# Oct 0's compact channels by staging copy and DMA transpose in difference form, with the DMA rates in the scheduler's model raised

## Chip, cores and metric

One core of a Trainium2 chip. The metric is the device time of one execution in microseconds (us), the median of several runs.

## The reference

A dilated causal convolution over time with a gated activation and a projection:

```python
# x (2, 16000, 144), w (15, 144, 288), w_o (144, 144), all bf16
dil, pad = 2, 28
xp = pad x with 28 zero rows ahead in time
h = sum over i in 0..14 of xp[:, pad - 2*i : pad - 2*i + T, :] @ w[i]     # 288 columns
z = tanh(h[..., :144]) * sigmoid(h[..., 144:])
return z @ w_o
```

## The kernel before

The 32000 time steps lie on 128 partitions, 250 steps each. One step of all partitions is a "tile" (128 rows); eight tiles are an "oct". The matmuls need the channels on the partitions, so every tile is transposed: channels 0 to 127 into XA, one tile each, and the last 16 channels ("compact channels", kept in XBc) packed eight taps to a 128-row tile, into XB. For fewer matmuls, differences of tiles and sums of weights are formed first (V, DU, DD, GU, GD, GX, GV from XA; WS, WC, WT from the weights), in the manner of a fast convolution.

All instructions are collected as operations with an estimated duration. A list scheduler inside the kernel's builder simulates the five engines and one DMA resource, and its simulated starts become the order in which each engine's instructions are emitted. An estimate in that model therefore never changes what is computed, but it changes the order.

Short names used below: "WS,GU matmuls" are those with WS as weights and GU as data; "XA<-STA" is an operation that reads STA and writes XA; a "bank copy" is a copy within PS, the accumulator memory; SPq and ACTq are the DMA queues of SyncE and ScalarE; ZT is the transposed Z, and OS holds the output before it is stored.

```python
DMA_RATE = 280e3
...
            if op.dma:                                   # in the scheduler's simulation
                t0 = max(dma_free, st + op.dur)
                turn = op.dma in ("xa", "xb", "zt")      # the DMA transposes
                dma_free = t0 + op.nbytes / (DMA_RATE * (0.6 if turn else 1.0))
                op.end = dma_free + (0.6 if turn else 2.3 if op.dma in ("xp", "wa", "wb") else 1.3)
...
        # compact channels of octs -1 and 0: TensorE transposes, ScalarE eviction
        for o, tiles, bb in ((-1, range(E0 - 4, E0), 7), (0, range(E0, E0 + 8), 6)):
            ...
            g.add("pe", fns, r=hk5 + ["XBcz", "ID"], alloc=[bk], dur=0.06 * len(fns))
            xb_op = g.add("act", ... activation(XB[:, bslot(o), i0:8, :], PSb[...], ACT.Copy), ...)
...
        def load_xb(o, parts=(0, 1)):                    # octs 1 and later
            for h in parts:
                def cp(v, h=h):                          # staging: XBc -> STB, 128x768
                    ...
                    return v.tensor_copy(dst, src) if o in BDVE else v.activation(dst, src, ACT.Copy)
                g.add("dve" if o in BDVE else "act", cp, ...)
            return g.add("sp", lambda e: e.dma_start_transpose(XB[:, s, :, :], STB[:, q, :, :]...),
                  r=[("STB", q, 0), ("STB", q, 1)], w=[("XB", s)], dur=1.7, dma="xb", ...)
```

"Staging" also exists for XA: a copy of Xr (the loaded x) into STA and a DMA transpose of 8 tiles. SyncE issues these transposes, the loads of Xr and the output stores from one queue, strictly in order.

## Time and profile before

| | before |
|---|---|
| time, median of 3 runs | 321.55 us (320.90 to 322.44) |
| span of the profiled run | 319.0 us |
| TensorE matmuls and transposes | 2643 in the profile, 2645 in the program |
| 100 to 280 us | TensorE never rests, full clock |

The profile is read in two layers. The page says who is busy; the chain and the starts of TensorE's instructions say who waits for whom. The lines that this rests on stand in the prediction below. One definition is used from here on. A **hole** is the time between the start of a group of TensorE instructions and the moment at which it could have started, which is the start of the group before it plus 0.123 us for each 288-column matmul in that group (0.057 us for each 128-column transpose).

### The profile page before, as it was taken

Reading aid. Unit: us, or ns where it says so; the run is one execution under the profiler, and the core shown is the slowest. Engines: PE = TensorE matmul, PEld = TensorE weight load, DVE = VectorE, ACT = ScalarE, POOL = GpSimd, SP = SyncE. Lnnn points to the kernel's source line nnn. Section 1 sums busy time; section 2 is a strip of 40 time slices with the busy share of each in tenths; the row PEclk is TensorE's granted clock in tenths of the full one; section 3 lists DMA queues with packets and bytes.
Section 4 is the critical chain, followed back from the end, with each engine's and each line's share of the span. In section 5 each row is a group of like instructions: output and inputs, shape, how many; then the busy total and the mean of one; then the engine's idle time right before and its main releaser. Section 6 shows DMA issues by size and latency. Waiting matters only on the chain.

```text
span 319.0 us, 6912 instructions
## 1 busy us (share of the span) xinstructions
PE 310.7 (97%) x2643; PEld 239.1 (75%) x2643; DVE 284.6 (89%) x615; ACT 267.5 (84%) x635; POOL 16.6 (5%) x29
## 2 busy tenths in 40 slices
PE   7999999999999999999999999999999999999994
PEld 6677667777777777777777777777777777777673
DVE  2999999999999998999989999898989989894774
ACT  3896699898897989989798897979889797788674
POOL 8106400000000000000000000000000000000000
PEclk9999999999999999999999999999999999999999
DMA  8699969949987592988949495894949477131553
GB/s 206 209 207 165 266 117 218 179 128 183 194 165 197 105 245 73 209 165 122 251 92 238 94 205 156 147 210 108 229 111 183 100 131 184 46 69 74 113 131 92
DMA packets 127821, 50.38 MB, mean 158 GB/s; under 512 B 119134, under 2 KB 121615, under 8 KB 127789
## 3 DMA queue, kind: packets, MB, share of 16 engines
q1 hardware_dynamic: 127273, 49.62, 74.1%
q0 software_dynamic: 512, 0.33, 0.4%
q8 instruction: 20, 0.33, 0.4%
q14 instruction: 12, 0.10, 0.1%
q10 hardware_dynamic: 4, 0.01, 0.0%
HBM read 11.82 MB, written 9.22 MB: 66 GB/s over the span
## 4 chain that ended last, share of the span: by engine, by line
PE 86%; ACT 7%; DMA 4%; SPq 1%; issue 1%; DVE 0%; ACTq 0%
PE PS L747 76%; PE PS L846 9%; DMA XA<-STA 2%; ACT STB L680 2%; DMA Xp<-in_x_dram 2%; ACT STA L659 1%; ACT TS L768 1%; SPq L479 1%; ACT TS L771 1%; ACT PS L905 1%; ACT XB L620 0%; SPq L491 0%; PE PS L579 0%; PE PS L877 0%; ACT XA L588 0%
## 5 line engine op out<-in xcount | busy, mean ns | idle before, releaser
L1026 DVE TENSOR_TENSOR Xp<-PS,UX 128x576 f32<-128x576 f32 x90 | 63.0, 751 | 16.7 <-PE PS L747 16.6
L747 PE MATMUL PS<-WB,XB 128*128 128x288 bf16 x260 | 72.1, 286 | 0.0
L1038 DVE TENSOR_TENSOR PS<-PS,Xp 128x576 f32<-128x576 f32 x90 | 68.4, 760 | 2.1 <-ACT OS L854 1.0
L747 PE MATMUL PS<-WA,GD 128*128 128x288 bf16 x360 | 70.0, 286 | 0.1
L768 ACT ACTIVATE TS<-PS 128x288 f16<-128x288 f32 x125 | 51.7, 413 | 13.3 <-PE PS L747 12.3
L854 ACT ACTIVATE OS<-PS 128x432 bf16<-128x432 f32 (+1 forms) x88 | 42.3, 489 | 14.0 <-PE PS L846 12.8
L771 ACT ACTIVATE TS<-PS 128x288 f16<-128x288 f32 x125 | 51.4, 411 | 0.0
L905 ACT ACTIVATE PS<-PS 128x288 f32<-128x288 f32 x120 | 46.3, 408 | 2.8 <-PE PS L747 2.8
L974 ACT ACTIVATE UX<-PS 128x576 f32<-128x576 f32 x60 | 39.2, 654 | 10.7 <-PE PS L747 10.4
L680 ACT ACTIVATE STB<-XBc 128x768 bf16<-128x768 bf16 x56 | 47.5, 854 | 0.0
L747 PE MATMUL PS<-WS,GU 128*128 128x288 bf16 x210 | 44.3, 287 | 0.0
L846 PE MATMUL PS<-WOR,ZT 128*128 128x144 bf16 (+1 forms) x322 | 42.4, 253 | 0.2 <-DVE Xp L1026 0.2
L747 PEld LDWEIGHTS PS<-WA,GD 128*128 128x128 bf16 x360 | 33.7, 98 | 11.4 <-DVE PS L1038 3.2
L776 DVE TENSOR_TENSOR Z<-TS 128x288 bf16<-128x288 f16 x125 | 36.9, 301 | 4.4 <-ACT TS L771 4.2
L747 PE MATMUL PS<-WC,XB 128*128 128x288 bf16 x120 | 34.3, 286 | 0.0
L846 PEld LDWEIGHTS PS<-WOR,ZT 128*128 128x128 bf16 x322 | 27.9, 98 | 6.6 <-ACT OS L854 0.5
L747 PE MATMUL PS<-WD,DD 128*128 128x288 bf16 x180 | 31.9, 286 | 0.2 <-ACT PS L905 0.2
L747 PE MATMUL PS<-WC,V 128*128 128x288 bf16 x180 | 30.6, 286 | 0.0
L747 PE MATMUL PS<-WA,DD 128*128 128x288 bf16 x180 | 30.6, 286 | 0.0
L747 PEld LDWEIGHTS PS<-WB,XB 128*128 128x128 bf16 x260 | 25.4, 98 | 6.7 <-ACT XB L620 0.3
L747 PE MATMUL PS<-WA,V 128*128 128x288 bf16 x118 | 25.7, 286 | 0.3 <-ACT PS L1111 0.3
L747 PE MATMUL PS<-WT,DU 128*128 128x288 bf16 x120 | 24.5, 286 | 0.0
(93 smaller groups left out, 459.4 us busy)
## 6 DMA issues: line engine op xcount, KB each, us to landing
Xr<-in_x_dram SPq DMA_DIRECT2D x15, 576.0 KB, 4.6
out_dram<-OS SPq DMA_DIRECT2D x30, 288.0 KB, 3.0
WA<-in_w_dram SPq DMA_DIRECT2D x3, 288.0 KB, 5.3
ZT<-Z SPq DMA_TRANSPOSE x32, 3.7
Xp<-in_x_dram SPq DMA_DIRECT2D x2, 252.0 KB, 5.4
XA<-STA SPq DMA_TRANSPOSE x30, 3.5
XB<-STB SPq DMA_TRANSPOSE x30, 4.4
Xp<-in_x_dram SPq DMA_DIRECT2D x1, 441.0 KB, 4.1
```

Of the source, the lines that this page charges most:

```text
L479: return e.dma_start(tile_ap, src)
L680: return v.tensor_copy(dst, src) if o in BDVE else v.activation(dst, src, ACT.Copy)
L747: return lambda t: t.matmul(bank(bk.b), lhsT=lhs(), rhs=rhs(), start=start, stop=True, skip_group_check=True)
L768: return a.activation(TS[:, s, 0, :, :], both(bk, 0, D), ACT.Tanh)
L771: return a.activation(TS[:, s, 1, :, :], both(bk, D, D), ACT.Sigmoid)
L776: return v.tensor_tensor(dst, TS[:, s, 0, :, :], TS[:, s, 1, :, :], ALU.mult)
L846: return t.matmul(PS[:, c0:c0 + n * D], lhsT=ZT[:, zt, blk, :], rhs=WOR[:, wi:wi + n, :].rearrange("p a b -> p (a b)"), start=first, stop= ...
L854: return e.tensor_copy(dst, src) if eng == "dve" else e.activation(dst, src, ACT.Copy)
L905: g.add("act", lambda e: e.activation(bank(bk.b + 1), bank(bk.b), ACT.Copy), w=[bk], dur=t_act(N2), prio=0)
L974: g.add("act", lambda e: e.activation(UX[:, k, u % NU, :, :], both(X, 0, N2), ACT.Copy), r=[X], w=[("UX", k, u % NU)], frees=[X], dur=t_ac ...
L1026: g.add("dve", lambda v, k=k, wi=wi, vb=vb, us=us: v.tensor_tensor(wslot(wi), both(vb, 0, N2), UX[:, k, us, :, :], ALU.add), r=[vb, ("UX", ...
L1038: return v.tensor_tensor(both(d, 0, N2), src, wslot(wi), ALU.add)
```

## The change

Its intent: oct 0 is treated like all later octs. The 8 TensorE transposes and the eviction go, two ScalarE copies and one DMA transpose of 12 tiles come. The matmuls of oct 0's outputs must then use the difference form (tiles already subtracted on XBc, and one shared tile), and the shared one is added to each output tile apart. Besides, the model's DMA rate for transposes rises from 0.6 to 0.68 of DMA_RATE.

```diff
-                dma_free = t0 + op.nbytes / (DMA_RATE * (0.6 if turn else 1.0))
+                dma_free = t0 + op.nbytes / (DMA_RATE * (0.68 if turn else 1.0))
...
+    SHX = ()
...
-        for o, tiles, bb in ((-1, range(E0 - 4, E0), 7), (0, range(E0, E0 + 8), 6)):
+        for o, tiles, bb in ((-1, range(E0 - 4, E0), 7),):
...
-        def direct_b(k, b):
-            e = H + k
-            g.add("pe", region(b, [lambda: xb_tile(e), lambda: xb_tile(e - 2)], [lambda: WB[:, 0, :], lambda: WB[:, 1, :]]), ...)
+        def rem(k, shared_too=True):
+            ...
+            out = [(lambda: XB[:, bslot(o), bb + (2 if j == 0 else 0) + r, :], (lambda: WB[:, 0, :]) if j == 0 else (lambda: WC[:, 2, 3, :]))]
+            if shared_too:
+                out.append((lambda: XB[:, bslot(o), bb + 4 + r, :], lambda: WB[:, 2, :]))
+            return out, [...]
+        def direct_b(k, b, shared_too=True):
+            tw, keys = rem(k, shared_too)
+            g.add("pe", region(b, [x[0] for x in tw], [x[1] for x in tw]), r=keys, w=[b.bk], ...)
+        g.add("act", lambda a: a.activation(WC[:, 2, 3, :], WB[:, 1, :], ACT.Copy, scale=-1.0), ...)   # moved up
+        diff_b("dve", 1, 9, hk5 + ["XBcz"], "XBd_h")                                                   # was ("dve", 3, 7, ...), later
+        load_xb(0)
...
+            if pi == 0 and q in SHX:              # an option of the kernel, off here: share one matmul of a pair
+                tw, keys = rem(k_of(q))
+                g.add("pe", region(_Half(bk, 0), [tw[1][0]], [tw[1][1]]), ...)
```

Cut: the slices that let load_xb serve oct -1 too, the choice of tiles in rem, moved lines, and two ordering constraints that tied the pair sums to the old eviction and are dropped.

## The prediction

> **What bounds the kernel now.** I read the page first (busy shares, the chain), then the windows, then the chain in order of time, and last the instructions of TensorE between 13 and 47 us. The page:
>
> ```profile
> PE 310.7 (97%) x2643; PEld 239.1 (75%) x2643; DVE 284.6 (89%) x615; ACT 267.5 (84%) x635; POOL 16.6 (5%) x29
> ...
> PE 86%; ACT 7%; DMA 4%; SPq 1%; issue 1%; DVE 0%; ACTq 0%
> ```
>
> TensorE is busy 97% of the span and carries 86% of the chain that ended last. The stretches say where the rest lies (columns: busy us and instructions of PE, PEld, DVE, ACT, POOL, then clock, DMA share, GB/s):
>
> ```profile
> 15.00:20.00 5.00, 5.00 (x41) 3.52 (x39) 5.00 (x17) 5.00 (x11) 0.00 (x0) 1.00 0.87 202
> 20.00:25.00 5.00, 4.67 (x39) 3.50 (x38) 4.70 (x13) 5.00 (x11) 0.00 (x0) 1.00 0.96 183
> 25.00:30.00 5.00, 5.00 (x43) 3.92 (x41) 5.00 (x14) 3.25 (x9) 3.27 (x6) 1.00 1.05 128
> 30.00:35.00 5.00, 5.00 (x43) 3.99 (x41) 4.86 (x9) 2.50 (x6) 5.00 (x11) 1.00 1.26 229
> ...
> 100.00:200.00 100.00, 100.00 (x843) 77.11 (x842) 93.81 (x202) 88.52 (x213) 0.00 (x0) 1.00 0.77 163
> 200.00:280.00 80.00, 80.00 (x678) 61.94 (x677) 74.18 (x153) 69.43 (x168) 0.00 (x0) 1.00 0.72 145
> ```
>
> From 100 to 280 us TensorE never rests at full clock; the chain shows there only pieces of "PE", with a period of 9.37 us (a 7.90 us piece begins at 99.67 + 9.37 = 109.04, and so on). Nothing but fewer matmuls can shorten that part. Waits are left in the first 50 us, where ScalarE is full from 15 to 25 us and the DMA engines from 15 to 40. There the chain is:
>
> ```profile
> 12.36 1.02 ACT XA L588
> 13.38 0.94 ACT STA L659
> 14.33 1.40 ACT XB L620 x2
> 15.73 0.31 ACT XBc L545
> ...
> 22.34 0.94 ACT STA L659
> 23.28 0.31 ACT PS L1111
> ...
> 23.64 4.11 PE PS L747 x32
> 27.79 6.12 DMA XA<-STA
> 33.93 0.76 DVE V L700 x2
> 34.69 0.69 DVE PS L1038
> 35.42 2.68 PE PS L747 x20
> ```
>
> Two things bind in turn: ScalarE's queue from 12.4 to 23.6 us, then one XA transpose by DMA that took 6.12 us to land, after which VectorE makes the differences that release TensorE at 35.42. "Busy" hides what this costs. Matmuls of 288 columns are 286 ns long but start 0.123 us apart (64 of them take 7.9 us), so a short hole does not show as idle time. Comparing start times with 0.123 us per matmul gives TensorE's holes: 0.17 us before 15.79, 0.11 before 16.39, 0.49 before 23.64, 0.26 before 35.42, 0.19 before 38.12, 0.51 around 42.3 to 42.7, 0.12 before 45.00, 0.34 before 46.33: 2.2 us in all, plus some under 0.1. That is all that a better start could still give behind 13 us; the tail after 297 us is the other loose part.
>
> **What the Trainium skill says.** "Perfetto Trace Analysis", section Identifying the Most-Contended Engine, says that matmul busy time is a poor measure because the instructions overlap; the 286 ns against 0.123 us above agree, so I count spacings. "TensorE: Matmul & The Clock Gate", section Back-to-back issue gap, gives N/2.4 + 2.5 ns alone (122.5 ns at 288 columns, 56 ns at 128) but 81 ns at 128 columns in a stream with weight loads; here the twelve 128-column transposes of XBc with their weight loads take 13.44 to 14.12 us, 0.057 us each, so this trace decides for the lower figure. "VectorE: DVE Perf Modes", section The three transpose paths, puts one 128x128 bf16 transpose at 390 ns on TensorE and 1309 ns by DMA. In bulk both differ here (0.057 us of TensorE's time; 4.4 us until a 12-tile DMA transpose lands), but the direction holds: the DMA's costs latency, not TensorE's time. "DMA: Bandwidth & Descriptors", section Issuing engines are not separate DMA queues, says DMAs from all engines share the same 16; the XA transpose that took 6.12 us, against a median of 3.5, was in flight with ten WOR loads from POOL, which fits.
>
> **The change part by part.** Oct 0's compact channels (the last 16 of 144) went as 8 TensorE transposes into a bank and one ScalarE eviction of 128x1024. They now go as all later octs do: two ScalarE copies into STB and a 12-tile DMA transpose, with the differences already taken on XBc.
>
> TensorE loses 8 transposes: 8 x 0.057 = 0.45 us. The matmuls stay in number: each of oct 0's eight output tiles took two with WB and takes two now (one with WB or its negative, one with the sum), because the shared one is added to each tile apart. By the instruction order, 2645 PE instructions become 2637, and 2329 of 288 columns remain 2329. All that follows oct 0 stays in the same PE order up to the last 20.
>
> ScalarE loses one eviction, 1.02 us long (0.95 of its queue), and gains two copies of 0.73 in the queue: +0.5 us net, in the stretch where it is on the path. The copies stand first, right after the XA eviction ends at 13.38, so the queue becomes: STB pair to 14.84, XB eviction of 512 (0.48) to 15.32, STA 0.95 to 16.27, tanh and sigmoid 0.60 to 16.87, two bank copies 0.59 to 17.46, compaction 0.31 to 17.77, STA to 18.73, STB pair to 20.19, STB pair to 21.65, bank copy to 21.95, negated WB 0.30 to 22.25.
>
> VectorE's difference covers 2x2x144 instead of 2x2x112, about +0.05 us, before 13.2 us, so the STB copy does not wait for it.
>
> DMA: one transpose of 12 tiles more (30 to 31, on 155 issues), near 15 us. It displaces little: the Xr load that was issued at 15.76 stands before it now and can run near 12 us.
>
> Now TensorE along its new order. Transposes (4 left) from 13.44 to 13.67, eight WA matmuls to 14.65, then WB with XB of oct -1, which needs the eviction that ends at 15.32: start 15.38, a hole of 0.73 (it was 0.17 at this place). Then 4 + 4 + 7 matmuls to 17.22, 30 with WA,V to 20.95 (their bank copies end at 17.2 and 17.5, a hole of 0.05), 8 to 21.93, a wait for the bank copy until 22.05 (0.12, was 0.49), 3 + 8 + 12 to 24.9, and 2 + 4 + 2 + 2 to 26.2. Next are the WS,GU matmuls, which need XB of oct 2 by DMA. Its staging ends at 21.65 (before 21.57), and it landed about 5 us later; I take 26.45, a hole of 0.25. From there to the WV matmuls are 37 x 0.123 = 4.55 us: 31.0. In the kernel before they started at 31.00. So by 31 us the 0.45 us saved is eaten by the dearer early wait.
>
> After that: the transpose of XA for oct 4, issued at 27.79 before, stands ahead of the XB of octs 3 and 4 now and is staged by about 24.2, so it should be issued near 25 us and land by 30. That takes away the hole of 0.26 and with it VectorE's lateness, which feeds the later holes (1.15 us from 38 to 47). The four STB copies of ScalarE that lie together at 41 to 46 us are also spread a little. I count half of the latter: -0.26 - 0.3. In the tail the last Z transposes now go before the last four projections but eight: some -0.1 of the final wait. Sum: 0 - 0.26 - 0.3 - 0.1 = -0.65, so 321.55 - 0.65 = 320.9 us.
>
> **The rivals.** First, ScalarE's +0.5 us is not absorbed and XB of oct 2 lands later than 26.45: DMA is at 87 to 126% of its mean share from 15 to 35 us, and 1.9 us of transposing (12 tiles of 32 KB at the 210 GB/s of those stretches) is added in front. Then the hole before WS,GU is 1 us or more: 321.9 to 322.5. For it speaks that the POOL loads, which wait for that transpose, woke at 26.73 before, just when TensorE needed it; against it that Xr's 576 KB leave earlier. Second, all 2.2 us of holes go, since the DMA order is better and VectorE is early: 0.45 + about 1.5 gives 319.6. Against it: the early hole of 0.73 is new and certain by the order. Third, the transfer is hidden and everything later re-forms, since the steady part sets its own pace: only the 0.45 us or nothing shows, 321.1 to 321.5. The changed DMA rate in the scheduler's model moves only VectorE's small operations in the steady part (Z products against compactions), where VectorE is off the chain (0%), so I expect none of it there.
>
> **Range and chances.** Every way lies within 1.5 us of 321, and the three runs before spread by 1.5 us by themselves. Range 319.8 to 322.1. Two per cent is 6.4 us, three times all holes after 13 us: faster 0.01, same 0.98, slower 0.01.
>
> **What would show it.** PE instructions down by 8; the 100 to 280 us windows unchanged; a hole of about 0.7 us before the first WB,XB matmuls at 15.4; the hole before WA,V at 22 us smaller; the first WS,GU matmuls near 26.5; no VectorE wait for XA near 33 us. I am wrong if WS,GU starts after 27.2, if XB of oct 0 lands after 22 us (its matmuls stand there), or if the 9.37 us period changes.

## The result, and the profile after

| | before | after |
|---|---|---|
| median of 6 runs each, same chip | 321.42 us (320.89 to 322.44) | 321.48 us (321.10 to 322.30) |
| ratio, 95% interval | | 0.9999 (0.9977 to 1.0021) |
| span of the profiled run | 319.0 us | 319.4 us |

No change can be told from these runs. The page after, in the form of the page before in the prediction (busy shares; engines of the chain):

```profile
PE 310.1 (97%) x2635; PEld 237.8 (74%) x2635; DVE 284.9 (89%) x615; ACT 267.8 (84%) x636; POOL 16.8 (5%) x29
...
PE 88%; ACT 5%; DMA 2%; DVE 1%; SPq 1%; issue 1%; ACTq 0%
```

Eight instructions fewer on TensorE, one more on ScalarE, as worked out. DMA's share of the chain fell from 4% to 2%: the XA transpose of oct 4 is gone from it, and VectorE has come in with 1%. The stretches of the kernel after (same columns as in the prediction) say where:

```profile
15.00:20.00 5.00, 4.45 (x37) 3.47 (x38) 4.92 (x17) 5.00 (x11) 0.00 (x0) 1.00 1.04 231
...
25.00:30.00 5.00, 4.36 (x36) 3.25 (x35) 4.98 (x14) 3.69 (x10) 3.50 (x7) 1.00 1.31 162
...
100.00:200.00 100.00, 100.00 (x843) 76.89 (x841) 94.22 (x202) 88.48 (x214) 0.00 (x0) 1.00 0.79 164
```

From 100 to 200 us the same 843 matmuls. Between 15 and 30 us there are two stretches where TensorE now loses more than half a microsecond. The two holes are these (TensorE's instructions in time; in brackets the idle time in front and who ended it):

```profile
15.55 0.67 PE L750 MATMUL PS<-WB,XB 128*128 128x288 bf16 x4 [0.57 <-ACT XB L621]
...
27.08 0.42 PE L750 MATMUL PS<-WS,GU 128*128 128x288 bf16 x2 [0.64 <-DVE GU L703]
```

The first was foreseen. The second was foreseen at a third of its size and with another cause; the chain of the kernel after shows what it waits for (start, length, who):

```profile
13.55 1.46 ACT STB L682 x2
15.01 0.49 ACT XB L621
...
25.24 0.62 DVE STB L682 x2
25.87 0.22 DVE Z L779
26.08 0.34 DVE GX L703
26.42 0.61 DVE GU L703
...
27.08 9.77 PE PS L750 x77
```

ScalarE's queue runs through the two new STB copies to the XB eviction that TensorE needs at 15.5. Further on it is VectorE's queue: two STB copies, a Z product and GX stand in front of the GU difference that the WS,GU matmuls read.

**The ledger.** I count from X, the start of the Xp transposes that wait for the first load, since the arrival of that load scatters from run to run (X was 9.98 to 11.11 us over all runs). Y is the start of the last group of four WC,GV matmuls at 303 us. A = Y - X is then the body, and B = span - Y the tail.

| us | before | after | difference |
|---|---|---|---|
| X | 10.29 | 10.46 | +0.17 |
| transposes on TensorE, 8 x 0.057 | | | -0.45 |
| holes from 12 to 33 us | 1.04 | 1.96 | +0.92 |
| holes from 33 to 62 us | 1.53 | 1.07 | -0.46 |
| A by the starts themselves | 292.82 | 292.76 | -0.06 |
| B, the tail | 15.89 | 16.18 | +0.29 |

The three middle rows add up to 0.0 against the -0.06 that the starts give. So the expected gain is not hidden behind something: it was made (-0.45 and -0.46) and given back in the two holes, and the tail took a little more.

A and B leave out two things: X, and the part of the device time that lies outside the span. A + B rose by 0.23 us, which is less than the scatter of single runs.

### The profile page after: what moved, and what is told of

Same layout as the page of the kernel before. It is cut to its first block, busy times and chain, and to the rows that moved or that the text cites. A ratio compares the mean times of both kernels' runs of the same rounds, so it can differ in the third digit from the quotient of the medians.

```text
span 319.4 us, 6898 instructions
## 1 busy us (share of the span) xinstructions
PE 310.1 (97%) x2635; PEld 237.8 (74%) x2635; DVE 284.9 (89%) x615; ACT 267.8 (84%) x636; POOL 16.8 (5%) x29
## 4 chain that ended last, share of the span: by engine, by line
PE 88%; ACT 5%; DMA 2%; DVE 1%; SPq 1%; issue 1%; ACTq 0%
PE PS L750 78%; PE PS L849 9%; DMA Xp<-in_x_dram 2%; ACT STB L682 2%; ACT STA L660 1%; SPq L480 1%; DVE Xp L1029 0%; ACT TS L774 0%; SPq L492 0%; ACT PS L935 0%; PE PS L580 0%; PE PS L880 0%; ACT PS L1134 0%; ACT XA L589 0%; ACT TS L771 0%
## 5 line engine op out<-in xcount | busy, mean ns | idle before, releaser
L1029 DVE TENSOR_TENSOR Xp<-PS,UX 128x576 f32<-128x576 f32 x90 | 63.1, 752 | 16.3 <-PE PS L750 16.1
L682 ACT ACTIVATE STB<-XBc 128x768 bf16<-128x768 bf16 x58 | 49.0, 853 | 0.0
L750 PE MATMUL PS<-WS,GU 128*128 128x288 bf16 x210 | 44.3, 287 | 0.6 <-DVE GU L703 0.6
L779 DVE TENSOR_TENSOR Z<-TS 128x288 bf16<-128x288 f16 x125 | 37.7, 303 | 4.7 <-ACT TS L774 4.2
L750 PE MATMUL PS<-WC,XB 128*128 128x288 bf16 x124 | 35.5, 286 | 0.0
L750 PEld LDWEIGHTS PS<-WB,XB 128*128 128x128 bf16 x256 | 24.9, 98 | 7.1 <-ACT XB L621 0.9
L750 PEld LDWEIGHTS PS<-WS,GU 128*128 128x128 bf16 x210 | 18.5, 98 | 8.3 <-DVE GU L703 0.9
```

What stands on the lines that cost most here:

```text
L750: return lambda t: t.matmul(bank(bk.b), lhsT=lhs(), rhs=rhs(), start=start, stop=True, skip_group_check=True)
L779: return v.tensor_tensor(dst, TS[:, s, 0, :, :], TS[:, s, 1, :, :], ALU.mult)
L1029: g.add("dve", lambda v, k=k, wi=wi, vb=vb, us=us: v.tensor_tensor(wslot(wi), both(vb, 0, N2), UX[:, k, us, :, :], ALU.add), r=[vb, ("UX", ...
```

## The experiments

Theory: (1) the saving on TensorE is given back at 15.5 us by ScalarE's queue and at 27 us by VectorE's order before GU; (2) the rate in the model acts through the order alone, and is not neutral; (3) the tail follows the order of the last output copies. Rivals: the hole at 27 us is the DMA's (XB of oct 2 late); the rate does nothing; ScalarE's extra time is absorbed.

| run | A | B | median | ratio to before (95%) |
|---|---|---|---|---|
| x1_rate | 297.56 | 16.19 | 325.61 | 1.0116 (1.0089 to 1.0144) |
| x2_chan | 294.61 | 15.92 | 322.88 | 1.0041 (1.0016 to 1.0066) |
| x3_gu | 292.70 | 16.19 | 321.37 | 0.9982 (0.9955 to 1.0009) |
| x6_dbl | 295.55 | 16.19 | 323.42 | 1.0050 (1.0019 to 1.0082) |
| x4_pool | 295.17 | 16.22 | 323.81 | 1.0054 (1.0011 to 1.0097) |
| x7_pool034 | 298.67 | 16.18 | 326.94 | 1.0151 (1.0108 to 1.0194) |
| x5_shx | 294.47 | 16.19 | 322.64 | 1.0020 (0.9978 to 1.0062) |
| x12_vlate | 294.29 | 16.17 | 323.15 | 1.0048 (1.0017 to 1.0079) |
| x9_tail | 292.84 | 16.60 | 321.71 | 0.9992 (0.9942 to 1.0041) |
| x11_tailpin | 292.80 | 16.02 | 321.32 | 0.9978 (0.9955 to 1.0001) |
| x10_best | 294.04 | 16.02 | 322.64 | 1.0022 (1.0001 to 1.0044) |
| x13_xr | 292.50 | 16.02 | 320.56 | 0.9962 (0.9939 to 0.9985) |

A and B are from one profiled run each; the median is of 4 to 6 runs, beside 7 to 12 of the kernel before on the same chip (medians 321.36 to 321.80). The intervals say which small differences are clear of noise. All outputs are right. The text compares A of x1_rate and x12_vlate with the kernel before (292.82) and A of the others with the kernel after (292.76).

The expectation was met in x12_vlate and x13_xr (the theory), x3_gu (its second rival) and x7_pool034 (the rival). In the other eight, A or B lies outside what theory and rival allowed. In x2_chan, x5_shx, x6_dbl and x4_pool, A came out 1.7 to 2.8 us above that of the kernel after, where a few tenths, or at most 1.5 us in x6_dbl, had been expected.

### The two parts of the change alone

**x1_rate**: the kernel before with the rate alone.

```diff
-                dma_free = t0 + op.nbytes / (DMA_RATE * (0.6 if turn else 1.0))
+                dma_free = t0 + op.nbytes / (DMA_RATE * (0.68 if turn else 1.0))
```

> The kernel before, with the DMA rate of the scheduler's model raised and nothing else; TensorE's order is that of before except in the tail, where the last four Z transposes stand ahead of the last projections as in the changed kernel. Two intervals of the trace are compared: A, from the eight Xp transposes that wait for the Xp load (10.29 us before, 10.46 after) to the last WC,GV matmuls (303.11 and 303.22), which was 292.82 us before and 292.76 after; B, from there to the end of the span, 15.89 before and 16.18 after. Theory (the tail's order is the rate's doing and costs 0.3 us because the first of three output stores is issued later): A 292.8 as before, B 16.1 to 16.2. Rival (B's difference is the scatter of a single DMA landing): B anywhere in 15.8 to 16.2, with its first store issued at the same distance as before (11.27 us after the WC,GV matmuls; after it was 11.52). Time within 0.3% of before in either.

Measured: slower by 1.2%, A + 4.74 us, although no instruction was added or removed. This profiled run is the slowest of the six (326.27). VectorE's instructions of this run show it:

```profile
34.90 0.42 DVE L700 TENSOR_TENSOR V<-XA 128x512 bf16<-128x512 bf16 x1 [2.34 <-DMA XA<-STA]
```

and its chain in order of time:

```profile
28.28 6.59 DMA XA<-STA
...
36.32 0.69 DVE PS L1047
...
37.06 3.43 PE PS L747 x14
```

The model, with its faster DMA, presumably takes XA of oct 4 to be there (its simulated times were not printed), and it places a V difference that reads it ahead of sums (L1026, L1047) that TensorE needs. In truth that transpose was issued at 28.28 us and landed 6.59 us later, as slow as before (6.12 us). VectorE works in order, so it stood for 2.34 us with ready work behind, and TensorE for 2.52 us. Then comes a second loss: the next 16 matmuls, from 37.06 to 40.70, take 3.64 us, 0.228 us each, nearly twice the usual spacing. (The 3.43 us in the chain are 14 of them up to the end of the last, so the 0.245 us of the expectation below is too high.) The window of 5 us shows a lowered clock (third column from the end):

```profile
35.00:40.00 5.00, 2.94 (x13) 1.84 (x14) 4.39 (x10) 1.10 (x3) 0.55 (x1) 0.72 0.89 284
```

The holes from 12 to 62 us are 3.2 us more than in the kernel before and the half-rate stretch loses 3.64 - 16 x 0.123 = 1.67 us: together 4.9, against 4.74 by the starts.

The second loss does not belong to every execution. The trace shows 3.41 us at half clock, which lowers the mean clock of a span of 324 us to 0.995 or less. The clocks of the six executions are 0.994 and 0.995 (326.27 and 326.06 us), but 0.997, 0.999, 1.000 and 1.000 (325.71, 325.51, 324.15 and 325.12 us): the last four cannot have had it. Without it, 4.74 - 1.67 = 3.07 us of A are left as the cost of the order.

**x12_vlate**: x1_rate with only those two V differences put back behind the sums.

```diff
         _ms = g.schedule()
+        lst = g.order["dve"]
+        for op in (g.ops[vf[4] + 1], g.ops[vf[4]]):      # the two V<-XA 128x512 of oct 4
+            lst.remove(op)
+            lst.insert(lst.index(l47[0]) + 1, op)        # behind the first L1047 sum
```

> The kernel before with the raised rate alone, in which VectorE stood 2.34 us at 32.5 us waiting for XA of oct 4 ahead of the sums that release TensorE; here the two V differences that read that XA stand behind those sums, as in the kernel before. All else as in that run. Theory (the 4.7 us that the rate alone cost are this one misplaced wait: a hole of 2.5 us, then 3.4 us of matmuls at half their rate, then VectorE late): the hole at 37 us shrinks to at most 1.2 us, no stretch of matmuls 0.245 us apart, A 293.2 to 294.6 instead of 297.56. Rival (the rate's other reorderings cost it): A above 296.

A fell from 297.56 to 294.29. The hole at 36 us is 0.57 instead of 2.52, and no matmuls run at half rate:

```profile
35.99 0.42 PE L749 MATMUL PS<-WA,GD 128*128 128x288 bf16 x2 [0.41 <-DVE PS L1042]
```

So in the profiled runs two misplaced instructions carry 3.3 of the rate's 4.7 us, half of it by the clock. By the ratios to the kernel before they carry 0.7 of the 1.2% (1.0116 against 1.0048, on two chips). The other 1.5 us lie mostly in holes of 0.58 at 39.5, 1.18 at 44.3 and 0.58 at 51.5 us; which of the other moves made these was not taken apart.

**x2_chan**: the kernel after with the rate left at 0.6.

> The changed kernel with the old DMA rate in the scheduler's model: the compact channels of oct 0 by staging and DMA, and the tail's order of before; the order around 17 to 33 us differs from the changed kernel's. Theory (the change of channels saves 0.45 us of TensorE and gives it back in two new holes, one before the first WB,XB matmuls of about 0.6 us, one of 0.6 before the first WS,GU): first hole again 0.5 to 0.7 us since the staging copies still stand ahead of the XB eviction, B back at 15.9, A 292.3 to 292.9. Rival (the new rate is what made the order worse, the channels alone would gain): A under 292.3, time under 321.0.

Slower by 0.4%. Here SyncE issues the two XA transposes behind a ZT transpose, at 26.07 us instead of 23.82, VectorE is behind, and TensorE has holes of 1.23 us at 36.45 (released by VectorE's L1050) and 0.91 at 44.83. So the two parts do not add: the channels alone +0.4%, the rate alone +1.2%, both 0.0%. In the changed kernel the XA transpose of oct 4 is issued near 25.3 us instead of 28.3, so the early V differences find their data and the trap of x1_rate stays shut (VectorE has no wait for XA there). x5_shx opens it again.

**x5_shx**: the kernel after with the option for shared matmuls turned on for two of the four pairs: two matmuls fewer.

```diff
-    SHX = ()
+    SHX = (2, 3)
```

> The changed kernel with the shared compact matmul of two of oct 0's four tile pairs added once to the pair's sum instead of to each tile apart: 2 matmuls of 288 columns fewer, 0.25 us of TensorE. Theory (TensorE's work before 27 us is not what holds the start; the waits on ScalarE and VectorE are): those 0.25 us only widen a hole, A within 0.15 of 292.76. Rival (work counts one for one): A 292.4 to 292.6.

Two matmuls are 0.25 us, yet A is 1.71 longer. In the new order that XA transpose is issued at 28.86 us and lands at 34.9. VectorE, in x5_shx:

```profile
34.94 0.43 DVE L703 TENSOR_TENSOR V<-XA 128x512 bf16<-128x512 bf16 x1 [1.97 <-DMA XA<-STA]
```

TensorE then has a hole of 1.95 us at 36.09. It is the instruction of x1_rate at the same place, reached by an edit that leaves the rate at 0.68. The interval of the time, 0.9978 to 1.0062, does not show that x5_shx is slower; the loss is read from the profile, and no run put the order back.

### The hole at 15.5 us: ScalarE's queue

**x6_dbl**: the kernel after with each of oct 0's two staging copies done twice on ScalarE (the extra copy goes into OS, which nothing reads yet): +1.46 us.

```diff
+                def cq(v, h=h):                     # the same copy, into unused space of OS
+                    ...
+                    return v.activation(dst, src, ACT.Copy)
-                g.add("dve" if o in BDVE else "act", cp, ...)
+                g.add("dve" if o in BDVE else "act", [cq, cp] if o == 0 else cp, ...)
```

> The changed kernel with each of the two ScalarE staging copies of oct 0 done once more into a buffer that is free then; orders otherwise identical, 1.46 us more of ScalarE at 13.5 us. Theory (ScalarE's queue is the path from 12.5 to 25 us, so what the change adds to it counts in full until a later wait absorbs it): the first WB,XB matmuls go from 15.55 to 17.0, WS,GU from 27.08 to about 28.0 to 28.5, A grows by 1.0 to 1.5 us, time by 0.3 to 0.5%. Rival (ScalarE has slack behind the first hole; TensorE's wait there comes out of a later wait): the first hole grows by 1.4 but WS,GU move by under 0.4 us and A by under 0.4.

A + 2.79 us, more than the 1.46 added. TensorE's instructions in x6_dbl:

```profile
17.16 1.14 PE L755 MATMUL PS<-WB,XB 128*128 128x288 bf16 x4 [2.06 <-ACT XB L621]
```

The hole grew from 0.72 to 2.22 us, the full added time, so ScalarE's queue is on the path at 15.5 us and absorbs nothing. After it 15 matmuls take 3.34 us (17.16 to 20.50), 0.223 each: another 1.5 us lost. The sum is 3.0; 0.13 of it comes back where the hole at 22 us vanishes. As in x1_rate, the second loss is not in every execution: three had clocks of 0.992 to 0.993 (the profiled one among them; 324.01 to 324.63 us), while three had 0.998 to 0.999, too high for such a stretch, and took 322.06 to 322.83 us.

**x4_pool**: oct 0's staging on POOL, which is idle there, instead of ScalarE; the scheduler is told 0.8 us per copy. **x7_pool034**: the same for octs 0, 3 and 4, which also takes the four copies from VectorE.

```diff
+    BPOOL = (0,)            # x7_pool034: (0, 3, 4)
-                    return v.tensor_copy(dst, src) if o in BDVE else v.activation(dst, src, ACT.Copy)
-                g.add("dve" if o in BDVE else "act", cp, ..., dur=0.27 if o in BDVE else 0.708, ...)
+                    return v.tensor_copy(dst, src) if o in BDVE or o in BPOOL else v.activation(dst, src, ACT.Copy)
+                g.add("pool" if o in BPOOL else "dve" if o in BDVE else "act", cp, ..., dur=0.8 if o in BPOOL else ...)
```

> The changed kernel with oct 0's two staging copies on the idle POOL engine instead of ScalarE; the scheduler is free to reorder. How long POOL takes for a 128x768 bf16 copy is not known (its 128x32 copy took 0.21 us). Theory (ScalarE's queue makes the hole of 0.72 us before the first WB,XB matmuls): these start at 14.6 to 14.9 with a hole under 0.3 us, and interval A (from the eight Xp transposes that wait for the load to the last WC,GV matmuls; 292.82 us before, 292.76 after) falls by 0.3 to 0.7. Rival (what is taken from ScalarE is paid by VectorE's queue, which is full from 12 to 46 us, or by XB of oct 0 coming late from a slow POOL copy): first hole gone, A within 0.25 of 292.76.

> As the run before in this group, and the four staging copies of octs 3 and 4 go from VectorE to POOL too, 1.2 us of VectorE at 25 to 28 us. Theory (from 27 to 43 us VectorE's queue holds TensorE, which is why the GU difference moved forward gave nothing): the holes at 27 and at 33 to 36 us shrink together to under 0.4 us and A falls to 291.8 to 292.4. Rival (POOL's two copies of oct 4 stand behind its sixteen WOR loads and come at 33 us, so XB of oct 4 lands late and a wait for it takes their place): A above 292.8, with a TensorE or SP wait on POOL.

In x4_pool the hole at 15.5 us shrank from 0.72 to 0.27, as it should when ScalarE's queue is freed. But a hole of 1.46 opened at 17.77, released by VectorE (a WS sum). VectorE's instructions beside the two POOL copies (13.86 to 16.05 us) in x4_pool:

```profile
14.04 1.31 DVE L704 TENSOR_TENSOR V<-XA 128x1024 bf16<-128x1024 bf16 x1
15.28 1.04 DVE L704 TENSOR_TENSOR DU<-XA 128x512 bf16<-128x512 bf16 x1
```

The same two forms take 0.69 and 0.42 us elsewhere, so each was held for 0.62 us; these 1.24 us are most of the hole of 1.46. The Trainium skill, "SBUF — State Buffer", section SBUF: two separate sides, says that a VectorE instruction with two SBUF inputs, as these are, and a GpSimd instruction that reads SBUF take a shared pair of ports as an exclusive lock for a whole instruction, and that the other fully blocks. These numbers agree, and x7_pool034 shows the other direction. Its staging copies (count: shortest, median and longest in ns):

```profile
L683 POOL COPY STB<-XBc x6: 835/1162/4187, 13.3 to 40.8; 128x768 bf16<-128x768 bf16 x6
```

One copy beside a full VectorE took 4.19 us, against 0.36 us for the same copy on VectorE. The XA transpose behind it came late, and TensorE had a hole of 2.63 us at 38.62, followed by 16 matmuls in 3.64 us: about half rate again. POOL looks free on the page (5%) and is not free beside VectorE.

### The hole at 27 us: VectorE's order

**x3_gu**: the kernel after, with the GU difference moved ahead of the two STB copies of that place.

```diff
         _ms = g.schedule()
+        d = g.order["dve"]
+        d.remove(gu0)
+        d.insert(d.index(stb3) - 1, gu0)
```

> The changed kernel with one VectorE instruction moved: the GU difference of the first pair stands ahead of a Z product, two STB copies, another Z product and GX (1.7 us) instead of behind them; all other orders are identical. Theory (the hole of 0.8 us before the first WS,GU matmuls at 27.08 is VectorE's GU, not the DMA of XB of oct 2): WS,GU start at 26.4 to 26.6, then held by the DMA transpose, and A falls by 0.4 to 0.6 us to 292.2 to 292.4. Rival 1 (the XB transpose lands just as late): WS,GU stay at 27.0, A unchanged. Rival 2 (the time is taken up by later holes at 35 to 43 us, where VectorE is behind): WS,GU early, A within 0.15 of 292.76.

TensorE in x3_gu has no idle time in front of these matmuls:

```profile
27.05 0.41 PE L750 MATMUL PS<-WS,GU 128*128 128x288 bf16 x2
```

The hole fell from 0.80 to 0.11 us: WS,GU starts at X + 15.94 instead of X + 16.62. So it was VectorE's order and not the DMA. But A moved by only -0.06. The STB copies and what follows them are later now, and new holes stand at 33.40 (0.34, released by VectorE's L1029), 35.41 (0.28) and 39.59 (0.23). VectorE has no slack between 25 and 40 us: moving one operation forward moves the wait to the next. The interval of the time, 0.9955 to 1.0009, contains no change.

### The tail

In every run B is the time from Y to the issue of the last three output stores (11.27 to 11.52 us) plus 4.6 to 4.7 us for these, except in x9_tail. Queue of SyncE in the kernel before, then in the kernel after:

```profile
314.38 1.65 SPq L822 DMA_DIRECT2D out_dram<-OS  x3
```

```profile
314.74 1.64 SPq L825 DMA_DIRECT2D out_dram<-OS  x3
```

That is Y + 11.27 and Y + 11.52. x1_rate has the late issue (11.52) without the new channels, x2_chan the early one (11.27) with them: the order of the tail comes from the rate.

**x9_tail**: the kernel after, with the very last store issued by ScalarE's queue, so that three issues of 0.5 us don't stand behind each other.

```diff
-        store_both("sp", o0, o1, dls[2:], 4)
+        store_both("act", o0, o1, dls[2:], 4)
```

> The changed kernel with its very last store issued by ScalarE, which has just made its data, instead of third in SP's queue; all else identical. Theory (the tail is bound by three stores issued one after the other by SP, 1.64 us from 11.52 us after the last WC,GV matmuls, so an earlier issue of the last shortens the end one for one): interval B (from those matmuls to the end of the span), 16.18 us, falls to 15.5 to 15.8; A unchanged. Rival (the three stores share the DMA engines, and the last lands when all are done, whoever issues it): B within 0.15 of 16.18.

Queue of ScalarE in x9_tail:

```profile
315.42 0.42 ACTq L825 DMA_DIRECT2D out_dram<-OS  x1
```

Its issue began at 315.42, some 0.4 us earlier than the third of the three issues in the kernel after (314.74 plus two thirds of 1.64 is 315.83), and yet B is 16.60, 0.4 longer, which neither theory nor rival allowed; why was not found. Issuing the last store sooner is not what shortens the tail.

**x11_tailpin**: the kernel after, with the order of the last Z transposes, their copies and the output copies put back as in the kernel before.

```diff
         _ms = g.schedule()
+        move("pe", sp_ops[3]["tr"], sp_ops[1]["mm"])     # last Z transposes behind the second last projection
+        move("act", sp_ops[3]["xa"], sp_ops[1]["os"])
+        ... the last two Z evictions of VectorE exchanged
```

> The changed kernel with the last four Z transposes and what follows from them put back in the order of before; nothing else. Theory (the store of the two first tiles waits for a ScalarE copy that the new order put behind three others, and the tail then runs at the DMA engines' pace): first store issued 11.2 to 11.3 us after the last WC,GV matmuls (11.52 in the changed kernel), B 15.85 to 15.95 instead of 16.18, A 292.7 to 292.9. Rival (B differs by chance of the last landing): B within 0.1 of 16.18.

B 16.02 instead of 16.18: 0.16 of the 0.29, with the first store at Y + 11.35. The rest stayed, since another pair of ScalarE's last operations kept its new order. The time, 0.9978 (0.9955 to 1.0001), is at the edge of what can be told.

### Putting it together

**x10_best**: GU forward (x3_gu), the tail pinned (x11_tailpin), and the STB copies of octs 3 and 4 moved from VectorE into gaps of ScalarE between 28 and 40 us, with the XB transpose of oct 4 later on SyncE, so that VectorE gets the room that x3_gu lacked.

```diff
+        for op in stb:                                   # four STB copies of octs 3 and 4
+            g.order["dve"].remove(op)
+            op.eng = "act"
+        a.insert(a.index(s1[0]) + 1, stb[0])
+        a.insert(a.index(ux[0, 1]) + 1, stb[1])
+        a.insert(a.index(ux[0, 1]) + 3, stb[2])
+        a.insert(a.index(ux[1, 0]) + 1, stb[3])
+        i = sp.index(xb4)
+        sp.insert(i + 4, sp.pop(i))
```

> The changed kernel with four pinned moves: the GU difference of the first pair forward on VectorE; the four staging copies of octs 3 and 4 from VectorE (25 to 28 us) into ScalarE's idle gaps at 29 to 36 us, with the XB transpose of oct 4 four places later on SP; and the tail's order of before. Theory (the hole before the first WS,GU matmuls and those at 33 to 36 us are one VectorE backlog of about 1.2 us; the end is set by the first output store): WS,GU 15.9 to 16.1 us after the Xp transposes that wait for the load (16.62 in the changed kernel, 15.94 with GU alone moved), no hole over 0.15 us from there to 38 us, interval A (from those Xp transposes to the last WC,GV matmuls) 291.9 to 292.3 instead of 292.76, B (from there to the end) 15.85 to 15.95 instead of 16.18; span about 0.9 us shorter, time ratio to before 0.996 to 0.999. Rival (the late holes re-form because ScalarE, now fuller, or XB of octs 3 and 4 is late at 43 us): A within 0.15 of 292.76.

The holes between 27 and 38 us went (0.14 at most), as intended, yet A is 294.04. VectorE's instructions in x10_best:

```profile
38.42 0.23 DVE L547 COPY XBc<-Xr 128x256 bf16<-128x256 bf16 x1 [1.39 <-DMA Xr<-in_x_dram]
```

and SyncE's queue, in its order:

```profile
31.48 1.43 SPq L687 DMA_TRANSPOSE XB<-STB  x1
32.95 1.02 SPq L480 DMA_DIRECT2D Xr<-in_x_dram  x1
```

The load of Xr stood behind the XB transpose of oct 3, whose staging now comes late. TensorE paid 1.45 us at 40.02, and later 0.4 us more where ScalarE waited for XB of oct 4.

**x13_xr**: x10_best with that one load in front of the XB transpose.

```diff
+        i = sp.index(xb3)
+        j = next(k for k in range(i, len(sp)) if sp[k].dma == "xr")
+        sp.insert(i, sp.pop(j))
```

> x10_best with one transfer moved: the first load of Xr behind the start is issued ahead of the XB transpose of oct 3 instead of behind it. In x10_best that load left at 32.95 us because the issuing queue stood at the late staging of oct 3; VectorE then waited 1.39 us for Xr at 38.4 and TensorE 1.45 us at 40.0. If that wait was the only price of x10_best's order, it goes: no VectorE wait for Xr, no hole above 0.4 us at 40 us, A (from the start of the third group of Xp transposes to the last group of projections) 292.0 to 292.6 against 294.04 in x10_best and 292.76 in the changed kernel, first output store 11.35 us after it as in x10_best, ratio to the kernel before 0.995 to 0.999. Rival: the work that ran late behind the Xr wait meets the next late transfer (XB of oct 4, for which ScalarE waited 0.60 us in x10_best) and the hole re-forms there: A 293 or more, ratio 1.000 or more.

SyncE's queue in x13_xr:

```profile
27.15 0.58 SPq L480 DMA_DIRECT2D Xr<-in_x_dram  x1
31.19 1.44 SPq L687 DMA_TRANSPOSE XB<-STB  x1
```

VectorE has no wait for Xr, the hole at 40 us is gone (0.22 at most between 27 and 42), and A is 292.50, within the expectation. The ratio to the kernel before is 0.9962 (0.9939 to 0.9985): the lowest ratio, and 0.4% or 1.1 us below the kernel before on this chip. The ledger explains little of that: against the kernel before A is shorter by 0.32 and B longer by 0.13, 0.19 us together. The rest lies in how the executions of the kernel before scatter (spans 318.9 to 321.6 us, and 318.7 to 319.2 for x13_xr) and in time outside the span; its cause is not shown. Against the kernel after x13_xr was not timed directly; A is shorter by 0.26 and B by 0.16.

## Why the prediction was right, and which of its steps were not

The predicted 320.9 us (319.8 to 322.1), with "within 2%" at 0.98, holds the measured 321.48. Of the six signs that it named, five came: 8 instructions fewer, an unchanged steady part, the hole of 0.7 us at 15.5, the smaller one at 22, no wait for XA near 33. WS,GU "near 26.5" did not. The frame was right: a steady part of 9.37 us periods that the change does not touch, and only about 2 us of holes to move.

- **TensorE, -0.45 us.** Right: 8 instructions fewer, and the ledger closes with 0.057 us each.
- **The first hole, 0.73 us.** Right: 0.72, at 15.55, released by the eviction behind ScalarE's two copies. x6_dbl shows that this queue binds.
- **The hole at 22 us, 0.12 instead of 0.49.** Right: 0.13.
- **"Next are the WS,GU matmuls, which need XB of oct 2 by DMA ... I take 26.45, a hole of 0.25."** This step failed. They started at 27.08 with a hole of 0.80, held by VectorE's GU difference; x3_gu removed it by moving that one operation. I had followed XB and not the other operand through VectorE's new order. The sum was off too: 24.9 plus ten matmuls is 26.1, not 26.2, so 26.45 meant a hole of 0.3. As a size: the WV matmuls were to start at 31.00 as before and started at 31.62, or 31.45 on the same X, so +0.45 us.
- **The XA transpose of oct 4 off the path, -0.26, and half of the later holes, -0.3.** About right: 1.53 us of holes behind 33 us became 1.07, -0.46, and VectorE no longer waits for XA.
- **The tail, -0.1.** Wrong in sign: +0.29. Moving the last Z transposes ahead delayed the last output copies, and with them the stores; x11_tailpin got 0.16 of it back by undoing the move.
- **"The changed DMA rate ... moves only VectorE's small operations in the steady part".** Wrong, and it cost nothing by luck. The rate alone costs 1.2% (x1_rate), since it moves V differences in the first 40 us. I had read the combined order, in which this does no harm, and taken it for a property of the rate.
- The rivals: the first (a dearer hole before WS,GU) comes near in effect (0.80 instead of 1 us or more, and 321.48 instead of 321.9) but not in cause; the third ("everything later re-forms") is what x3_gu showed when the hole was repaired alone.
- Two readings of the profile were off and carry little: the DMA column of the windows is the packets' time as a share of 16 engines' time, not a share of a mean; and 14 WOR loads, not ten, were issued from 26.73 us until the XA transpose of 27.79 us landed.

The failed step (0.45) and the tail (0.29 instead of -0.1, so 0.39) make 0.84 us; the prediction stood 0.58 below the median. What is between the two is less than the scatter of single runs, which is over 1 us for either kernel.

Not settled: what makes up the remaining 1.5 us of the rate's own cost (x12_vlate), which of the moves in x2_chan costs its 1.85 us of A over the kernel after, and why ratios move by a few tenths of a per cent that A and B do not show: A + B is 308.71 us before and 308.82 in x11_tailpin, whose ratio is 0.9978.

## What to carry to other kernels

Where a scheduler's model sets the order, a change of an estimate is a change of the kernel: test it apart from the part it came with, because two parts can each be slower alone and neutral together. For an engine that works in order, ask of every operation placed early whether its input is really there, and follow all operands of the next matmul through the new order, not the one that was late before. When an engine without slack holds up another, moving one operation forward only passes the wait on; room has to be made on that engine, and then the queue that feeds it has to be checked too, as x10_best and x13_xr show.

## What the Trainium skill lacked or had wrong

- "TensorE: Matmul & The Clock Gate", section Why this matters for your kernels, asks for no idle gaps over about 3 us between bursts. In the profiled runs, gaps of 2.22, 2.52 and 2.63 us (x6_dbl, x1_rate, x7_pool034) were each followed by 3.41 us at half clock, with matmuls 0.22 to 0.23 us apart instead of 0.123, and gaps of 1.95 us and less (x5_shx) were not. That costs about 1.5 to 1.7 us on top of the gap. The length of the slow stretch does fit the page's window of about 3.4 us. Length alone may not decide: in these three traces the clock fell after 10.24, 30.72 and 34.13 us at full clock, which are 3, 9 and 10 times 3.413 us, so it may matter where a gap lies on that grid. At least four of x1_rate's six executions and three of x6_dbl's had no slow stretch; their gaps were not traced.
- The same page, section Back-to-back issue gap: 81 ns for 128 columns in a stream with weight loads; here 57 ns, the page's own isolated figure.
- "VectorE: DVE Perf Modes", section The three transpose paths: 1309 ns for one 128x128 tile by DMA. A transpose of 12 tiles landed here in 3.7, 5.0 and 7.6 us (shortest, median, longest) and not in 12 times that figure; the page has no landing time for many tiles in one DMA, and none for how far it spreads.
- "SBUF — State Buffer", section SBUF: two separate sides: right on the lock, without durations for copies on POOL. Here a 128x768 bf16 copy took 0.84 to 1.29 us, and 4.19 us beside a full VectorE.
